# Two half stores of dV in uneven shares: some rows issued from GpSimd, with tiny loads that turn its cursor

## The chip, the cores and the metric

The kernel runs on one core of a Trainium2 chip. Its compute engines are TensorE (PE in the profile, with the weight loads as PEld), VectorE (DVE), ScalarE (ACT) and GpSimd (POOL); SyncE (SP) issues transfers and computes nothing. Sixteen DMA engines move data between HBM and the core's memory, whatever engine issued the transfer. The metric is the time of one execution in device microseconds, lower is better. A profiled execution gives, beside its time, a span (from the first to the last recorded instruction), the busy time of each engine and the records of the DMA packets.

## The reference

One query row attends to 8192 keys in each of 32 heads, and the gradients of all three inputs are wanted:

```python
B, H, Sq, Skv, Dh = 1, 32, 1, 8192, 128
scores = jnp.einsum('bhqd,bhkd->bhqk', q, k) * scale
attn = _softmax(scores, axis=-1)
out = jnp.einsum('bhqk,bhkd->bhqd', attn, v)
# outputs: out, dq, dk, dv  (vjp of the above with grad_out)
```

All arrays are bf16. K, V, dK and dV are 2 MB a head. With p the softmax row and ds the gradient of the scores, dV of a head is the outer product of p and grad_out, and dK that of ds and q. So 128 MB of K and V are read, and as much of dK and dV is written.

## The kernel before

The work goes head by head. A head's 8192 keys lie on 128 partitions, 64 keys each, so that one partition's part of a 2 MB tensor is a single run of 16 KB in HBM. A load of K or V (`load_k` L81, `load_v` L85) is one transfer of 128 rows of 16 KB.

For each head, in the loop at the end of the kernel: DVE transposes K in blocks (L162) and PE forms the scores (L177); softmax follows on DVE and ACT; PE transposes V (L197), ACT copies it out of PSUM (L188), and PE forms grad_out times V (L207). `contract` (L231) adds up the output and, with ds, dQ. `outer` (L256) writes dK and dV: DVE multiplies a repeated p or ds with a row, in four quarters of 16 keys per partition, into a tile of the pool `gen`, which holds two tiles each for dK and dV. After the fourth quarter, one transfer from SP stores all of it (L266); heads 0 and 31 store it in two halves. Iteration h of the loop does the scores and the softmax of head h, the dK of head h - 1 and the dV of head h.

K has three tiles and V two. K of head h + 2 is loaded once PE has finished the dQ of head h - 1 (the wait is on L231), V of head h + 2 once PE has read V of head h (L197 and L231). In the program the V load stands between the third and the fourth quarter of dV, and SP takes its transfers strictly in that order:

```python
        outer(h, "dv", 2)
        if 0 < h and h + 2 < H:
            load_v(h + 2)
        outer(h, "dv", 3)
```

The order is written out by hand (`manual_schedule`), and only the waits are added from what each instruction reads and writes. Eight completion semaphores go round over the transfers of SP and ACT, so that a transfer also waits for the one that had its semaphore before it. A tile of `gen` is written again two heads later, once its store has landed. GpSimd does a few memsets at the start and nothing else; all transfers are issued from SP, but for two small loads from ACT. At the very end the output and dQ are stored (`result`, L302).

Of the kernel before, what the change touches and what calls it, by code (L numbers as in the profile page):

```python
# [11 lines left out]
BF16 = mybir.dt.bfloat16  # L12
# [7 lines left out]
K_BUFS = 3  # L20
V_BUFS = 2
QD = 32


@with_exitstack
def kernel(
# [11 lines left out]
    nc = tc.nc  # L38
    P = 128
# [3 lines left out]
    NCH = NT // CH  # L43
    NQ = P // QD
    assert NCH == 4 and NQ == 4
    W = D // 2
    NB = W // QD
    scale = float(D) ** -0.5

    consts = ctx.enter_context(tc.tile_pool(name="consts", bufs=1))  # L50
# [18 lines left out]
    def rows_of(x, h, c, parts):  # L69
        L = NT // parts  # L70
        return x[0, h].rearrange("(p n) d -> p n d", p=P)[:, c * L:(c + 1) * L, :]

    def slots(X, c, parts):
        L = NT // parts
        return X[:, c * L:(c + 1) * L, :]

    def load_k(h):
        Kt[h] = kpool.tile([P, NT, D], BF16, tag="K", name="Kt")
        parts = NCH if h == 0 else 1
        for c in range(parts):  # L80
            nc.sync.dma_start(slots(Kt[h], c, parts), rows_of(k, h, c, parts))  # L81

    def load_v(h):
        Vt[h] = vpool.tile([P, NT, D], BF16, tag="V", name="Vt")
        nc.sync.dma_start(Vt[h][:], rows_of(v, h, 0, 1))  # L85
# [5 lines left out]
    load_v(0)  # L91
    load_k(1)
    load_v(1)

    ident = consts.tile([P, P], BF16)
    make_identity(nc, ident[:])
# [5 lines left out]
    nc.vector.memset(ones_f[:], 1.0)  # L102
    do_win = consts.tile([P, H, 2, QD + 2], BF16)
    nc.gpsimd.memset(do_win[:], 0.0)
    wins = {}
    for which in ("p", "ds"):
        wins[which] = []
        for i in range(2):
            w = consts.tile([P, NG, 2 * QD - 4], BF16, name=f"win_{which}{i}")
            nc.gpsimd.memset(w[:], 0.0)  # L110
            wins[which].append(w)
    q_win = []
    for i in range(2):
        w = consts.tile([P, 2 * NB, P + QD], BF16, name=f"win_q{i}")
        nc.gpsimd.memset(w[:], 0.0)
# [5 lines left out]
    q_blk = consts.tile([P, H, 2 * NB, NQ], BF16)  # L121
    four = consts.tile([H, 2 * NB, NQ, QD], BF16)
    for w in range(NB):
# [116 lines left out]
    def gather(h, which, bank):  # L240
# [5 lines left out]
                             start=(j == 0), stop=(j == 3), skip_group_check=True)  # L246
        nc.scalar.copy(to[:, h - ST + 1:h + 1], bank[:, at:at + ST])

    def outer(h, which, r):
        x = st[h]  # L250
        if r == 0:
            x[which] = gpool.tile([P, NT, D], BF16, tag=which, name="G_" + which)
        G, dst = x[which], out_2 if which == "dk" else out_3
        rep, row = x["ds"] if which == "dk" else x["p"], qd[h][:, 0 if which == "dk" else 1, :]
        Q = NT // 4
        nc.vector.tensor_tensor(  # L256
            slots(G, r, 4).rearrange("p n (a b) -> p n a b", b=R),
            slots(rep, r, 4).unsqueeze(2).to_broadcast([P, Q, D // R, R]),
            row.rearrange("p (a b) -> p a b", b=R).unsqueeze(1).to_broadcast([P, Q, D // R, R]),
            op=ALU.mult)  # L260
        parts = 1
        if h == 0 or h == H - 1:
            parts = 2
        if r % (4 // parts) == 4 // parts - 1:
            c = r // (4 // parts)
            nc.sync.dma_start(rows_of(dst, h, c, parts), slots(G, c, parts))  # L266
# [37 lines left out]
    for h in range(H + 1):  # L304
# [18 lines left out]
        if h > 0:  # L323
            ds_of(p_)
            outer(p_, "dk", 0)
            dq_of(p_, 0)
        if h < H:
            s_back(h)
        if h > 0:
            dq_of(p_, 1)  # L330
            outer(p_, "dk", 1)
            if p_ % ST == ST - 1:
                gather_copy("ds")
                gather(p_, "ds", st[p_]["m"])
# [9 lines left out]
        if h > 0:  # L344
            outer(p_, "dk", 2)
# [83 lines left out]
```

## Time and profile before

| | |
|---|---|
| time, median of 3 runs | 642.42 us (642.1 to 642.49) |
| the profiled execution's own time | 642.33 us |
| its span | 640.5 us |
| moved by DMA | 269.01 MB, mean 420 GB/s |
| DVE busy | 546.7 us (85%) |
| PE busy | 466.5 us (73%) |
| ACT busy | 205.5 us (32%) |
| POOL busy | 7.1 us (1%) |
| a 2 MB dV store, issue to landing | 34.8 us (median) |
| a 2 MB K load, issue to landing | 31.6 us (median) |

Busy time is the time in which an instruction of the engine ran; a DMA share is the mean over the sixteen DMA engines, so that one engine alone makes 0.06. "Landing" is when the last of a transfer's sixteen shares has arrived; the trace holds a completion record for each share, 4 bytes long, so that one can see how far apart the engines finish one transfer. The chain of waits is followed back from the last instruction to what released it. A 2 MB transfer puts eight rows of 16 KB on each DMA engine, and each engine works through its own queue.

### The profile page before, as it was taken

Reading aid. Unit: us, or ns where it says so; the run is one execution under the profiler, and the core shown is the slowest. Engines: PE = TensorE matmul, PEld = TensorE weight load, DVE = VectorE, ACT = ScalarE, POOL = GpSimd, SP = SyncE. Lnnn points to the kernel's source line nnn. Section 1 sums busy time; section 2 is a strip of 40 time slices with the busy share of each in tenths; the row PEclk is TensorE's granted clock in tenths of the full one; section 3 lists DMA queues with packets and bytes.
Section 4 is the critical chain, followed back from the end, with each engine's and each line's share of the span. In section 5 each row is a group of like instructions: output and inputs, shape, how many; then the busy total and the mean of one; then the engine's idle time right before and its main releaser. Section 6 shows DMA issues by size and latency. Waiting matters only on the chain.

```text
span 640.5 us, 8426 instructions
## 1 busy us (share of the span) xinstructions
PE 466.5 (73%) x3336; PEld 276.5 (43%) x3336; DVE 546.7 (85%) x780; ACT 205.5 (32%) x507; POOL 7.1 (1%) x13
## 2 busy tenths in 40 slices
PE   3776778778877867887866867767877687676771
PEld 1444444445544533455533444434554344444351
DVE  6799999998999999988889888898888988889871
ACT  1433332234433322334421333313442133322240
POOL 4000000000000000000000000000000000000000
PEclk9979888887787899877899887898787888879875
DMA  8999999999999999999999999999999999999994
GB/s 353 421 415 427 429 431 426 425 433 426 429 431 427 429 431 427 430 429 429 431 427 432 428 425 437 427 424 436 428 425 435 428 426 434 426 430 433 427 405 193
DMA packets 19671, 269.01 MB, mean 420 GB/s; under 512 B 2352, under 2 KB 2352, under 8 KB 2864
## 3 DMA queue, kind: packets, MB, share of 16 engines
q1 hardware_dynamic: 19536, 268.46, 98.6%
q8 instruction: 26, 0.43, 0.3%
q14 instruction: 13, 0.11, 0.0%
q10 hardware_dynamic: 96, 0.02, 0.0%
HBM read 134.23 MB, written 134.23 MB: 419 GB/s over the span
## 4 chain that ended last, share of the span: by engine, by line
DMA 45%; DVE 39%; PE 9%; ACT 4%; issue 1%; DVEq 0%; ACTq 0%
DMA Kt<-in_k_dram 45%; DVE XK_sb L162 15%; DVE G_dv L256 9%; DVE G_dk L256 7%; PE s_ps L177 3%; DVE dpT L214 2%; PE T_ps L197 2%; PE acc_ds L231 2%; ACT XV_sb L188 2%; DVE sT L184 1%; ACT p_rep L371 1%; DVE prod L217 1%; DVE ds L285 1%; ACT qd L273 1%; DVE four L125 1%
## 5 line engine op out<-in xcount | busy, mean ns | idle before, releaser
L197 PE MATMUL T_ps<-ident_f,Vt 128*128 128x128 f32 x1024 | 178.0, 339 | 1.0 <-DMA Vt<-in_v_dram 0.4
L256 DVE TENSOR_TENSOR G_dv<-p_rep,qd 128x2048 bf16<-128x2048 bf16 x128 | 148.2, 1220 | 35.3 <-DMA out_dram<-G_dv 28.1
L177 PE MATMUL s_ps<-XK_sb,win_q 128*128 128x512 bf16 x512 | 135.8, 397 | 50.1 <-DVE XK_sb L162 26.3
L197 PEld LDWEIGHTS T_ps<-ident_f,Vt 128*128 128x128 f32 x1024 | 151.4, 177 | 28.5 <-issue 20.1
L256 DVE TENSOR_TENSOR G_dk<-ds_rep,qd 128x2048 bf16<-128x2048 bf16 x128 | 154.7, 1210 | 1.1
L188 ACT COPY XV_sb<-T_ps 128x512 f32<-128x512 f32 x256 | 138.4, 586 | 53.2 <-PE T_ps L197 52.6
L162 DVE STREAM_TRANSPOSE XK_sb<-Kt 128x1024 f32<-128x1024 f32 x128 | 151.4, 1221 | 3.1 <-DMA Kt<-in_k_dram 2.9
L177 PEld LDWEIGHTS <-win_q 128*128 128x128 bf16 x512 | 52.7, 105 | 123.8 <-issue 83.2
L290 ACT COPY win_ds<-ds 128x64 bf16<-128x64 bf16 x32 | 7.8, 244 | 193.0 <-DVE ds L285 193.0
L355 ACT ACTIVATE e<-sT,nbias 128x64 f32<-128x64 f32 x32 | 13.0, 406 | 138.4 <-DVE nbias L350 138.4
L343 PE MATMUL m_ps<-ident_f,top 128*128 128x128 f32 x32 | 11.0, 342 | 60.3 <-DVE top L341 57.3
L207 PE MATMUL dp_ps<-XV_sb,do_win 128*32 128x512 bf16 x512 | 34.0, 382 | 24.7 <-ACT XV_sb L188 24.7
L231 PE MATMUL acc_p<-Vt,win_p 128*32 128x512 bf16 x512 | 48.3, 516 | 0.5 <-ACT win_p L372 0.5
L343 PEld LDWEIGHTS m_ps<-ident_f,top 128*128 128x128 f32 x32 | 4.5, 139 | 74.4 <-DVE top L341 72.9
L231 PE MATMUL acc_ds<-Kt,win_ds 128*32 128x512 bf16 x512 | 33.5, 382 | 0.9 <-ACT win_ds L290 0.9
L207 PEld LDWEIGHTS <-do_win 128*32 128x32 bf16 x512 | 14.2, 94 | 36.0 <-issue 29.5
L369 DVE RECIPROCAL rinv<-m_ps 128x1 f32<-128x1 f32 x32 | 5.4, 168 | 24.9 <-ACT qd L273 24.9
L184 DVE STREAM_TRANSPOSE sT<-s_ps 128x512 f32<-128x512 f32 x32 | 22.7, 709 | 3.6 <-PE s_ps L177 3.6
L356 PE MATMUL m_ps<-rs,ones_f 128*128 128x1 f32 x64 | 15.4, 310 | 11.5 <-ACT e L355 11.5
L231 PEld LDWEIGHTS <-win_p 128*32 128x32 bf16 x512 | 13.1, 117 | 23.8 <-issue 12.2
L214 DVE STREAM_TRANSPOSE dpT<-dp_ps 128x512 f32<-128x512 f32 x32 | 21.6, 675 | 0.8 <-PE dp_ps L207 0.8
L356 PEld LDWEIGHTS m_ps<-rs,ones_f 128*128 128x128 f32 x64 | 14.0, 272 | 17.8 <-ACT e L355 17.3
(57 smaller groups left out, 203.3 us busy)
## 6 DMA issues: line engine op xcount, KB each, us to landing
Vt<-in_v_dram SPq DMA_DIRECT2D x32, 2048.0 KB, 29.5
Kt<-in_k_dram SPq DMA_DIRECT2D x31, 2048.0 KB, 31.6
out_dram<-G_dv SPq DMA_DIRECT2D x30, 2048.0 KB, 34.8
out_dram<-G_dk SPq DMA_DIRECT2D x30, 2048.0 KB, 32.2
out_dram<-G_dv SPq DMA_DIRECT2D x4, 1024.0 KB, 11.6
out_dram<-G_dk SPq DMA_DIRECT2D x4, 1024.0 KB, 11.7
Kt<-in_k_dram SPq DMA_DIRECT2D x4, 512.0 KB, 5.6
out_dram<-fin_sb SPq DMA_DIRECT2D x2, 8.0 KB, 12.1
```

Of the source, the lines that this page charges most:

```text
L162: nc.vector.transpose(XK[h][:, :, :, u, :], slots(Kt[h], u, NCH).rearrange("p g d -> p (g d)").bitcast(F32).rearrange("p (g w j) -> p g w ...
L177: nc.tensor.matmul(st[h]["s"][:], lhsT=q_win[h % 2][:, c, at:at + P], rhs=cols[:, c // 2, u, c % 2], start=(u == 0 and c == 0), stop=(u == ...
L184: nc.vector.transpose(sT[:].rearrange("p g r -> p (g r)"), x["s"][:])
L188: nc.scalar.copy(XV[h][:, c * TB:(c + 1) * TB, :], st[h].pop(("T", c))[:])
L197: nc.tensor.transpose(T_ps[:, i, :], words[:, m * P:(m + 1) * P], ident_f[:])
L207: nc.tensor.matmul(out[b * QD:(b + 1) * QD, :], lhsT=do_win[:, h, e2, 2 - 2 * z:2 - 2 * z + QD], rhs=cols[:, z, e2, :, b * QD:(b + 1) * QD ...
L214: nc.vector.transpose(x["dpT"][:].rearrange("p m r -> p (m r)"), x["dp"][:])
L231: nc.tensor.matmul(acc[which][b * QD:(b + 1) * QD, :], lhsT=window(h, which)[:, g, at:at + QD], rhs=X[:, 4 * g:4 * g + 4, :].rearrange("p ...
L256: nc.vector.tensor_tensor(slots(G, r, 4).rearrange("p n (a b) -> p n a b", b=R), slots(rep, r, 4).unsqueeze(2).to_broadcast([P, Q, D // R, ...
L343: nc.tensor.transpose(x["m"][:, 128:256], top[:].to_broadcast([P, P]), ident_f[:])
L355: nc.scalar.activation(e[:].rearrange("p (u g) -> p u g", u=NCH), x["sn"], ACT.Exp, bias=nbias[:], scale=scale, accum_out=rs[:])
L356: nc.tensor.matmul(x["m"][:, 0:1], lhsT=ones_f[:], rhs=rs[:], start=True, stop=True, skip_group_check=True)
```

## The change

dV of heads 10 and 16 is no longer stored in one transfer after its fourth quarter. Its first half (L256's first two quarters) is stored from SP as soon as it is there, as 128 rows of 8 KB. The second half goes in pieces, named by rows (partitions) in the table `UNEVEN`. For head 10: rows 0 to 56 from SP, 57 to 94 and 95 to 127 from GpSimd. For head 16: rows 0 to 119 from GpSimd, 120 to 123 and 124 to 127 from SP. Between them GpSimd issues loads of a few bytes per row into a tile that nobody reads, of 7 and 12 rows at head 10 and of 5 and 12 at head 16 (`turn`). GpSimd's stores are cut into pieces of at most 4096 bytes. The bytes stored and all computing instructions stay what they were.

```diff
+UNEVEN = {
+    10: (("sync", 0, 57), ("turn", 7, 0), ("pool", 57, 95), ("turn", 12, 0), ("pool", 95, 128)),
+    16: (("turn", 5, 0), ("pool", 0, 120), ("turn", 12, 0), ("sync", 120, 124), ("sync", 124, 128)),
+}
...
+    turns = list(range(8))
+    turned = consts.tile([16, len(turns), 2, 2], BF16)
...
+    def turn(n):
+        i = turns.pop()
+        nc.gpsimd.dma_start(turned[0:n, i], k[0, 0].rearrange("(p n) d -> p n d", p=P)[0:n, 0:2, 0:2])
+
+    def spread(h, c, dst, G):
+        if c == 0:
+            nc.sync.dma_start(rows_of(dst, h, 0, 2), slots(G, 0, 2))
+            return
+        for what, a, b in UNEVEN[h]:
+            if what == "turn":
+                turn(a)
+            elif what == "sync":
+                nc.sync.dma_start(rows_of(dst, h, 1, 2)[a:b], slots(G, 1, 2)[a:b])
+            else:
+                nc.gpsimd.dma_start(rows_of(dst, h, 1, 2)[a:b], slots(G, 1, 2)[a:b], max_dma_last_dim=4096)
...
             op=ALU.mult)
+        if which == "dv" and h in UNEVEN:
+            if r % 2 == 1:
+                spread(h, r // 2, dst, G)
+            return
         parts = 1
```

## The prediction

> **What bounds the kernel now.** I read the page's DMA rows first, then the chain, then the DMA share by stretch, then the trace's completion records of single transfers.
>
> ```profile
> span 640.5 us, 8426 instructions
> ...
> DMA  8999999999999999999999999999999999999994
> ...
> q1 hardware_dynamic: 19536, 268.46, 98.6%
> q8 instruction: 26, 0.43, 0.3%
> ...
> DMA 45%; DVE 39%; PE 9%; ACT 4%; issue 1%; DVEq 0%; ACTq 0%
> ```
>
> The DMA engines are full in every slice but the first and the last. DVE, the busiest compute engine, is at 85%. The chain runs over DVE in its first part and from 251.94 us on over K loads of some 32 us each, one for two heads: early on the kernel lives on loads made ahead, later on what the DMA engines deliver. The trace's packets say how full: a 16 KB row takes 611 ns (median), an 8 KB row 309, a 4 KB one 159, a completion record of 4 bytes 9, and from 20 to 600 us sixteen packets, one per engine, are under way all the time. So an engine with more to do, or a slower one, ends later, and nothing evens that out. The share by stretch shows that this is so at the end (columns: stretch, its length, the engines' busy time, the TensorE clock, DMA share, GB/s):
>
> ```profile
> 400.00:600.00 200.00, 147.53 (x1052) 86.68 (x1052) 170.52 (x242) 63.34 (x156) 0.00 (x0) 0.86 1.01 429
> 600.00:616.00 16.00, 11.83 (x74) 6.40 (x74) 13.23 (x22) 4.10 (x10) 0.00 (x0) 0.83 1.01 431
> 616.00:625.00 9.00, 6.17 (x58) 4.44 (x58) 6.95 (x11) 3.62 (x9) 0.00 (x0) 0.88 0.90 375
> 625.00:631.00 6.00, 1.69 (x8) 1.40 (x8) 2.45 (x3) 0.64 (x3) 0.00 (x0) 0.50 0.96 399
> 631.00:632.00 1.00, 0.00 (x0) 0.00 (x0) 0.00 (x0) 0.00 (x0) 0.00 (x0) 0.50 0.50 203
> 632.00:634.00 2.00, 0.00 (x0) 0.00 (x0) 0.00 (x0) 0.00 (x0) 0.00 (x0) 0.50 0.24 99
> 634.00:636.00 2.00, 0.00 (x0) 0.00 (x0) 0.00 (x0) 0.00 (x0) 0.00 (x0) 0.50 0.12 50
> 636.00:639.00 3.00, 0.00 (x0) 0.00 (x0) 0.00 (x0) 0.00 (x0) 0.00 (x0) 0.50 0.06 25
> ```
>
> The last three shares are four, two and one sixteenth: from 636 us a single engine works, and everything waits for it. The sixteen completion records of the last transfer (the dQ store, issued at 627.90) agree: twelve at 631.59 to 632.39, then 634.35, 635.19, 635.72 and 639.47. The dV store of head 30 (issued at 599.24), where no engine has yet run dry, sorts the engines better: five at 612.91 to 613.60, one at 615.34, six at 617.25 to 617.62, three at 619.80 to 620.96, one at 624.51. Five fast, ten between, one slow, 11.6 us behind the first. The slow one loses steadily: about 0.15 us at each 2 MB store and 0.03 at each load. The middle ones lag in steps of some 1.45 us, one at each of the 26 instruction packets of q8; the fast ones show almost none.
>
> The lag also reaches the compute. K of head 31 lands last on the slow engine, and the work of that head follows:
>
> ```profile
> 567.39 31.98 DMA Kt<-in_k_dram
> 599.40 3.50 DVE XK_sb L162 x3
> ```
>
> Its records run from 588.58 to 596.62 for fifteen engines, and to 599.38 for the last one.
>
> **The change part by part.** *Where the rows go.* The two second halves give every engine 16 rows of 8 KB before (two halves, 128 rows each, 8 on each of 16 engines, as every 128-row transfer of the trace has 16 completion records). How a count that 16 does not divide is shared out, no row of this trace shows. The bounds: at most those 16 rows leave an engine, 16 x 0.309 = 4.94 us; at most one engine takes the largest single transfer that need not be even, 57 rows, 57 x 0.309 = 17.6 us, less the 16 it had, 12.7 us more. Both ends are kept for the rivals. The value I take comes from the counts themselves: 57 + 38 is 5 x 19, 33 is 11 x 3, 120 is 15 x 8, 4 is 4 x 1; shares of equal size on as many engines as divide the count. I read SP's transfers as starting at engine 0 and `turn(n)` as moving GpSimd's cursor by n, from 0. Head 10: SP's 57 rows put 19 on engines 0, 1, 2; the cursor at 7 puts 19 on 7 and 8; at 9 + 12 = 21, that is 5, the 33 put 3 on each of 5 to 15. Head 16: from 5 on, 8 rows on fifteen engines, all but 4; SP's two fours put one row twice on 0 to 3. Against the 16 of before: engines 0 to 2 +13, 7 and 8 +14, engine 3 -6, 5, 6 and 9 to 15 -5, engine 4 -16. Five get more, ten a little less, one far less: the same five, ten and one as in the records. I cannot see engine numbers there, but this match is why I take engine 4 for the slow one and the value near the lower bound.
>
> *The slow engine:* 16 rows less, -4.94 us, 639.47 to 634.53. *The next three:* -5 rows, -1.55 us, 635.72 to 634.17; they stay just under. *The five fast:* +14 x 0.309 = 4.33 us. They run dry at the end (share 0.90 at 616 to 625): after 617.75 they have four 1 MB stores left, 32 x 0.309 = 9.9 us, so even without a pause they end at 617.75 + 9.9 + 4.3 = 632, under 634.5. *Compute:* K of head 31 lands at the later of 599.38 - 4.94 = 594.44 and 596.62 - 1.55 = 595.07, 4.3 us sooner; the last stores are issued by about 623.2 instead of 627.5 and do not decide.
>
> *Smaller rows:* the first halves go as 8 KB rows, 309 ns for what was 611 / 2 = 305.5: 16 x 3.5 ns = 0.06 us on each engine. GpSimd's rows are cut into two 4 KB pieces, 318 for 309: 0.2 us on engines 7 and 8 alone. *The four tiny loads:* a few pieces of 4 bytes on an engine, between 9 ns (completion record) and 18 ns (256-byte row): under 0.1 us.
>
> *GpSimd's issue.* POOL is idle after 7.6 us, and the seven transfers stand at its end with a wait on DVE at the first store of each head; nobody queues behind. Making such a transfer has no row here: between the 0.33 us of an SP issue and the 1.92 us of POOL's longest instruction, for each of two or three. It is hidden, as the rows are needed only when the buffer comes round two heads later: dV of head 10 is issued at 209.29, and head 12 first writes the buffer at 239.8. By the lag at 233 us (fast 0, slow 5.04) engines 0 to 2 with 11 rows more in that half land it at 233.2 + 3.4 = 236.6, still in time. If that cover fails, DVE waits; a few us at head 12 are given back, since the engines still hold some 30 us of work.
>
> *SP.* The first half is issued before the V load of head h + 2 instead of behind it: V lands 8 x 0.309 = 2.5 us later. V of head 12 landed at 233.4 and is first used at 236.1, so that is covered; V of head 18 landed at 351.3 and is used at 351.4, so PE waits some 2.4 us there, and the queues go on meanwhile. One transfer more at head 10 and two at 16: eight completion semaphores go round, so each transfer waits for the one eight places before it. After head 16 I get, by the landings of before: the second four-row store waits for dK of 14 (326.6 against 321.6), K of 19 is issued at 331.5 instead of 329.4, dV of 17 at 346.4 instead of 341.3. The engines then still hold 15 us or more of queued rows (V of 19 lands from 364.7 on), so 0 on the path; were the queue to run dry, up to 5 us.
>
> The sum, on the profiled execution's own 642.33 us (span 640.5), 0.09 under the median 642.42: -4.94 + 0.06 + 0.1 = -4.8, **637.5 us**.
>
> Against it stands a rule of the Trainium skill, page "DMA: Bandwidth & Descriptors", "Rules for kernel authors": spreading transfers over issuing engines gains no bandwidth, as all run on the same 16. By it alone the sum would be 0 and the time 642.4; but the tail row at 0.06 share is not one of bandwidth, it is one engine's own queue.
> The same page, "Why a DMA increments its semaphore by 16", says that the largest divisor up to 16 sets the number of engines, lowest first from SP and from a round-robin cursor on GpSimd, with a measured exception for some GpSimd copies, shared out over all 16; by the exception the cursor would do nothing and engine 4 lose 2 rows, 641.7. Its "Latency and other measured facts" calls engines 7 and 15 usually slower; were 7 the slow one, +14 rows would give 646.7. No row here numbers the engines.
>
> **The rivals.**
> - *The slow engine is one of the five that get more* (cursor or numbers not as I read them). For: no engine number is in the trace. Against: the five, ten and one. +13 to +14 rows: 639.47 + 4.0 to 4.3, so 646.4 to 646.7, slower (the far end, +12.7 us, would be 655). It decides as soon as the slow engine takes 5 rows more than before (1.5 us).
> - *The slow engine is in the middle group:* -5 rows, 640.9; or one of the next three gets +14: 635.72 + 4.33 = 640.1, which is no longer the end unless its step falls later. 640 to 643.
> - *The counts come out nearly even,* the cursor has no effect: one or two rows either way, 641.7 to 642.7.
> - *A stall:* the semaphore turn or a late buffer lets the queues run dry; 2 to 5 us on top of no gain, 643.5 to 647.
>
> **How the numbers follow.** A measurement of this kernel can tell about 0.2%, 1.3 us. As read: 0.64, 636.4 to 638.8 (the next three unrelieved would give 642.4 - 3.75 = 638.7). Middle group: 0.14, of it 0.08 faster, 0.03 same, 0.03 slower. Slow engine loaded: 0.12, slower. Even: 0.06, of it 0.02 faster, 0.04 same. Stall: 0.04, slower. Faster 0.74, same 0.07, slower 0.19. From 636.4 to 643.3 lie the first, the second and the fourth, 0.84.
>
> **What would show it.** Right: the DMA share falls off around 631 to 634.5 with no stretch of 3 us at 0.06; the latest record of head 30's dV is about 6.7 us behind the first five's old place, not 11.6; K of 31 lands near 595. Wrong: a longer lone tail after 636, or the same one; DVE waiting on the dV stores of 10 or 16; a DMA share under 0.9 anywhere in 200 to 600.

## The result, and the profile after

The changed kernel takes 639.53 us (median of 6 runs, 639.15 to 639.86) where the kernel before took 642.45 beside it. The ratio is 0.9955, interval 0.9942 to 0.9968: 2.9 us faster, where 4.9 were forecast. The profiled execution took 639.71 us with a span of 637.9; before it was 642.33 and 640.5, so that it shows 2.6 us.

From the page of the changed kernel, the span, the DMA engines' busy share in 40 slices, the queues (packets, MB, share of sixteen engines) and the shares of the chain of waits:

```profile
span 637.9 us, 8444 instructions
...
DMA  8999999999999999999999999999999999999996
...
q1 hardware_dynamic: 19612, 266.90, 98.5%
q0 software_dynamic: 1136, 1.57, 0.7%
q8 instruction: 26, 0.43, 0.2%
...
DMA 41%; DVE 39%; PE 11%; ACT 5%; issue 1%; POOL 0%; DVEq 0%; ACTq 0%
```

The DMA engines are as full as before. Queue q0 is new and is GpSimd's: 1.57 MB, the 191 rows of 8 KB of its three stores, 382 pieces of 4 KB; the other 754 of its packets are of 4 or 8 bytes. The other engines do what they did. The last slice rose from 4 to 6 tenths: the end is sharper.

The DMA share by stretch at the end of the changed kernel (columns as in the prediction):

```profile
600.00:616.00 16.00, 12.14 (x95) 7.55 (x96) 13.22 (x22) 6.06 (x14) 0.00 (x0) 0.89 1.01 429
616.00:625.00 9.00, 6.06 (x44) 3.85 (x36) 7.75 (x12) 1.85 (x7) 0.00 (x0) 0.63 0.99 422
625.00:631.00 6.00, 0.24 (x1) 0.05 (x1) 0.00 (x0) 0.25 (x1) 0.00 (x0) 0.50 0.93 389
631.00:632.00 1.00, 0.00 (x0) 0.00 (x0) 0.00 (x0) 0.00 (x0) 0.00 (x0) 0.50 0.55 231
632.00:634.00 2.00, 0.00 (x0) 0.00 (x0) 0.00 (x0) 0.00 (x0) 0.00 (x0) 0.50 0.32 132
634.00:636.00 2.00, 0.00 (x0) 0.00 (x0) 0.00 (x0) 0.00 (x0) 0.00 (x0) 0.50 0.12 50
636.00:639.00 3.00, 0.00 (x0) 0.00 (x0) 0.00 (x0) 0.00 (x0) 0.00 (x0) 0.50 0.01 3
```

From 636 us on a share of 0.06, one engine, has become 0.01. But in 632 to 634 it is 0.32, five sixteenths, where it was 0.24: more engines end late. The completion records of the dV store of head 30, as us behind the first of its sixteen engines, show the whole field (from the traces; first 612.91 before, 612.82 after):

```
before 0.00 0.04 0.07 0.09 0.69 2.43 4.34 4.51 4.64 4.68 4.70 4.71 6.89 7.54 8.05 11.60
after  0.00 2.30 2.33 2.43 3.38 4.17 4.34 4.38 4.86 4.95 5.36 6.17 7.09 7.90 7.92  9.31
```

Of the five engines that came first one leads alone, the others have joined the middle, and the 11.60 is gone. The last place, 9.31, belongs to another engine. It can be followed from transfer to transfer by its steps at four instruction packets (28, 208, 401 and 591 us), and before it was one of the next three. On the last transfer (dQ) it ends at 636.91; the formerly slow engine ends at about 635.83 there, and at 639.47 before.

Two lines of the chain of waits after, K of head 31 and the work that follows it:

```profile
565.20 32.62 DMA Kt<-in_k_dram
597.84 3.50 DVE XK_sb L169 x3
```

Its load was issued 2.19 us sooner than before (565.20 for 567.39) but took 32.62 us instead of 31.98, and landed 1.6 us sooner (597.82 for 599.38).

### The profile page after: what moved, and what is told of

The parts are those of the page before. It is cut to its first block, busy times and chain, and to the rows that moved or that the text cites. A ratio compares the mean times of both kernels' runs of the same rounds, so it can differ in the third digit from the quotient of the medians.

```text
span 637.9 us, 8444 instructions
## 1 busy us (share of the span) xinstructions
PE 470.7 (74%) x3336; PEld 277.4 (43%) x3336; DVE 546.7 (86%) x780; ACT 205.5 (32%) x507; POOL 11.7 (2%) x20
## 3 DMA queue, kind: packets, MB, share of 16 engines
q0 software_dynamic: 1136, 1.57, 0.7%
## 4 chain that ended last, share of the span: by engine, by line
DMA 41%; DVE 39%; PE 11%; ACT 5%; issue 1%; POOL 0%; DVEq 0%; ACTq 0%
DMA Kt<-in_k_dram 29%; DVE XK_sb L169 13%; DVE G_dv L279 11%; DVE G_dk L279 8%; DMA out_dram<-G_dv 5%; DMA Vt<-in_v_dram 5%; PE s_ps L184 4%; PE T_ps L204 3%; ACT XV_sb L195 2%; DVE dpT L221 2%; DVE sT L191 2%; PE acc_ds L238 1%; ACT p_rep L398 1%; PE m_ps L383 1%; PE acc_p L238 1%
## 5 line engine op out<-in xcount | busy, mean ns | idle before, releaser
L184 PE MATMUL s_ps<-XK_sb,win_q 128*128 128x512 bf16 x512 | 138.4, 410 | 40.4 <-DVE XK_sb L169 23.4
L238 PE MATMUL acc_p<-Vt,win_p 128*32 128x512 bf16 x512 | 51.0, 540 | 0.9 <-ACT win_p L399 0.9
L214 PEld LDWEIGHTS <-do_win 128*32 128x32 bf16 x512 | 14.2, 94 | 36.0 <-issue 29.4
L238 PEld LDWEIGHTS <-win_p 128*32 128x32 bf16 x512 | 13.4, 120 | 25.3 <-issue 14.2
## 6 DMA issues: line engine op xcount, KB each, us to landing
Kt<-in_k_dram SPq DMA_DIRECT2D x31, 2048.0 KB, 30.8
out_dram<-G_dv POOLq DMA_DIRECT2D x1, 960.0 KB, 18.3
```

The source lines that it names most:

```text
L184: nc.tensor.matmul(st[h]["s"][:], lhsT=q_win[h % 2][:, c, at:at + P], rhs=cols[:, c // 2, u, c % 2], start=(u == 0 and c == 0), stop=(u == ...
L214: nc.tensor.matmul(out[b * QD:(b + 1) * QD, :], lhsT=do_win[:, h, e2, 2 - 2 * z:2 - 2 * z + QD], rhs=cols[:, z, e2, :, b * QD:(b + 1) * QD ...
L238: nc.tensor.matmul(acc[which][b * QD:(b + 1) * QD, :], lhsT=window(h, which)[:, g, at:at + QD], rhs=X[:, 4 * g:4 * g + 4, :].rearrange("p ...
```

## The experiments

All kernels store everything that the changed kernel stores; they differ in the table `UNEVEN`, but for one with another piece size. The kernel before ran beside each of them, with medians of 642.45 to 642.54. Where "long packets" are given, the length of every packet above the median length of its size (611 ns for 16 KB, 309 for 8, 159 for 4, 9 for a completion record) is summed over the sixteen engines, instruction packets left out, in three stretches of the trace: 205 to 255 us (after head 10's store), 320 to 360 (head 16's), 438 to 490 (head 22's). The last record and the long packets are those of the one profiled execution, whose time is up to 0.9 us off the kernel's median; the same store of head 10 shows 10.2 to 17.5 us of long packets in five traces, so that smaller differences say little. "Slow engine" is the one that was last before.

| kernel | median us | ratio (interval) | last record, dQ | long packets, us |
|---|---|---|---|---|
| before | 642.45 | | 639.47 | 3.8 / 2.8 / 2.9 |
| changed kernel | 639.53 | 0.9955 (0.9942 to 0.9968) | 636.91 | 10.2 / 15.2 / 2.5 |
| head 10 alone | 640.07 | 0.9959 (0.9947 to 0.9972) | 637.61 | 16.2 / 2.6 / 2.0 |
| head 16 alone | 640.40 | 0.9966 (0.9954 to 0.9979) | 637.51 | 3.0 / 22.8 / 2.1 |
| GpSimd, 128 rows | 642.15 | 0.9994 (0.9985 to 1.0003) | 639.39 | 9.0 / 1.8 / 2.0 |
| engine 5 left out | 641.87 | 0.9990 (0.9981 to 0.9999) | 639.00 | 3.3 / 13.8 / 2.2 |
| two halves from SP | 641.58 | 0.9986 (0.9978 to 0.9995) | 638.98 | 5.7 / 1.9 / 1.9 |
| pieces of 8 KB | 642.04 | 0.9994 (0.9985 to 1.0002) | 639.83 | 33.3 / 15.2 / 2.1 |
| uneven from SP | 641.70 | 0.9991 (0.9982 to 1.0) | 639.37 | 2.8 / 3.5 / 2.6 |
| two skips | 640.84 | 0.9975 (0.9966 to 0.9984) | 638.38 | 28.9 / 24.3 / 2.5 |
| 64 + 64 rows from GpSimd | 643.32 | 1.0016 (1.0007 to 1.0026) | 640.27 | 24.8 / 17.2 / 2.0 |
| changed kernel again | 640.12 | 0.9958 (0.9946 to 0.9971) | 637.49 | 13.7 / 11.6 / 2.5 |
| head 22 for head 16 | 639.42 | 0.9951 (0.9938 to 0.9963) | 636.59 | 16.4 / 2.6 / 10.3 |
| head 10's way twice | 640.06 | 0.9968 (0.9957 to 0.998) | 638.14 | 17.5 / 2.6 / 8.0 |

### One head at a time

```diff
 UNEVEN = {
     10: (("sync", 0, 57), ("turn", 7, 0), ("pool", 57, 95), ("turn", 12, 0), ("pool", 95, 128)),
-    16: (("turn", 5, 0), ("pool", 0, 120), ("turn", 12, 0), ("sync", 120, 124), ("sync", 124, 128)),
 }
```

> Only head 10 is stored unevenly; head 16 as before. Theory A (the lone slow engine sheds 8 rows of 309 ns a head, 2.47 us; part of the gain is lost to packets that run longer than 611 ns around the GpSimd stores): the slow engine still ends last, 642.4 - 2.5 + 0.4 = 640.3 us. Rival B (GpSimd's way of storing has a fixed price of some 0.95 us a head, whatever it relieves): 642.4 - 2.5 + 0.95 = 640.9. Rival C (another engine takes over as the last as soon as the slow one is relieved by 8 rows): one head brings as much as both, 639.5.

And head 16 alone:

```diff
 UNEVEN = {
-    10: (("sync", 0, 57), ("turn", 7, 0), ("pool", 57, 95), ("turn", 12, 0), ("pool", 95, 128)),
     16: (("turn", 5, 0), ("pool", 0, 120), ("turn", 12, 0), ("sync", 120, 124), ("sync", 124, 128)),
 }
```

> Only head 16 is stored unevenly; head 10 as before. Theory A: the slow engine sheds 2.47 us; the packets around the stores of head 16 were longer by some 12 us summed over 16 engines, 0.7 us each, so 642.4 - 2.5 + 0.7 = 640.6 us, and in the records around 330 to 345 us the long packets come again. Rival B: 640.9, with no long packets. Rival C: 639.5.

The DMA share by stretch, head 10 alone:

```profile
634.00:636.00 2.00, 0.00 (x0) 0.00 (x0) 0.00 (x0) 0.00 (x0) 0.00 (x0) 0.50 0.09 37
636.00:639.00 3.00, 0.00 (x0) 0.00 (x0) 0.00 (x0) 0.00 (x0) 0.00 (x0) 0.50 0.02 8
```

Head 16 alone:

```profile
634.00:636.00 2.00, 0.00 (x0) 0.00 (x0) 0.00 (x0) 0.00 (x0) 0.00 (x0) 0.50 0.12 49
636.00:639.00 3.00, 0.00 (x0) 0.00 (x0) 0.00 (x0) 0.00 (x0) 0.00 (x0) 0.50 0.01 6
```

Either head takes 8 rows, 2.47 us by the rows, from the slow engine, and either gains about that: 2.38 and 2.05 us. In both the slow engine still comes last, at 637.61 and 637.51, 1.9 to 2.0 us sooner than before. Together they would be worth 4.4, near the forecast; the changed kernel gains 2.9. So each part does its work, and the second one finds less left to win: another engine ends then.

### Which engine is relieved

Head 16 alone, with the cursor one place further, so that engine 5 is left out of the 120 rows and engine 4 isn't:

```diff
-    16: (("turn", 5, 0), ("pool", 0, 120), ("turn", 12, 0), ("sync", 120, 124), ("sync", 124, 128)),
+    16: (("turn", 6, 0), ("pool", 0, 120), ("turn", 11, 0), ("sync", 120, 124), ("sync", 124, 128)),
```

> Head 16 alone as in the run of head 16 alone, but the cursor is turned one further (by 6, and by 11 afterwards), so that engine 5 is left out of the 120 rows and engine 4 has its 8. If engine 4 is the slow one (theory A): no relief, 642.4 + 0.7 = 643.1 us, and the last records stay some 11.6 us behind the first. If the slow engine's number is not known by this (rival: any engine left out would do, or the slow one is 5): 640 to 640.6.

```profile
634.00:636.00 2.00, 0.00 (x0) 0.00 (x0) 0.00 (x0) 0.00 (x0) 0.00 (x0) 0.50 0.13 54
636.00:639.00 3.00, 0.00 (x0) 0.00 (x0) 0.00 (x0) 0.00 (x0) 0.00 (x0) 0.50 0.05 19
```

These are its last two stretches: at 636 to 639 us 0.05 for the 0.01 of head 16 alone. The slow engine ends at 639.00, and the time is 641.87 against 640.40. One place of the cursor is worth 1.5 us, so the slow engine is the one that `turn(5)` spares. The expectation had 643.1 us for this case; why it is 0.6 us faster than before, and not 0.7 slower, stays open. The Trainium skill, page "DMA: Bandwidth & Descriptors", section "Why a DMA increments its semaphore by 16 and not by 1", has GpSimd's shares on consecutive engines from a round-robin cursor, and SP's on the lowest; on that numbering it is engine 4. Its section "Latency and other measured facts" calls 7 and 15 usually slower; no run here shows that.

### GpSimd without uneven shares

```diff
-    10: (("sync", 0, 57), ("turn", 7, 0), ("pool", 57, 95), ("turn", 12, 0), ("pool", 95, 128)),
-    16: (("turn", 5, 0), ("pool", 0, 120), ("turn", 12, 0), ("sync", 120, 124), ("sync", 124, 128)),
+    10: (("pool", 0, 128),),
+    16: (("pool", 0, 128),),
```

> The second halves of heads 10 and 16 go from GpSimd as 128 rows each, 8 on every engine: the GpSimd way without any shift of rows. Theory A: no relief, and only the longer packets: 642.4 + 0.5 to 1.1 = 642.9 to 643.5 us. Rival B: the price of the way alone, 642.4 + 1.9 = 644.3. If the loss in the changed kernel came from the uneven shares and not from GpSimd: 642.4 to 642.6.

642.15 us, within what can be told from no change and under what any of the expectations had, and the slow engine ends at 639.39, as before. The issuing engine alone gives nothing; the gain is in the counts. This is what the rule in the Trainium skill's "Rules for kernel authors" (same page) says of spreading transfers over issuing engines, and the changed kernel's 2.9 us are no breach of it: no stretch before the end moves more bytes.

### SP without GpSimd

The second halves from SP as one transfer of 128 rows each, and the same for head 16 in 68 + 60 rows, which leaves fewer rows on the engines behind the fourth:

```diff
-    10: (("sync", 0, 57), ("turn", 7, 0), ("pool", 57, 95), ("turn", 12, 0), ("pool", 95, 128)),
-    16: (("turn", 5, 0), ("pool", 0, 120), ("turn", 12, 0), ("sync", 120, 124), ("sync", 124, 128)),
+    10: (("sync", 0, 128),),
+    16: (("sync", 0, 128),),
```

> Heads 10 and 16 stored from SP in two halves of 128 rows each, 8 rows a half on every engine; no GpSimd, no uneven shares. Shows what the split, the V load behind the first half and the extra turn of the semaphores cost by themselves. Theory A (the loss comes from longer packets around the GpSimd store of head 16 and from another engine ending last): 642.4 to 642.6 us, no cluster of packets over 1 us near 330 us. Rival C2 (the split and the delayed issues on SP cost the missing time): 643 to 644.4.

```diff
-    10: (("sync", 0, 57), ("turn", 7, 0), ("pool", 57, 95), ("turn", 12, 0), ("pool", 95, 128)),
-    16: (("turn", 5, 0), ("pool", 0, 120), ("turn", 12, 0), ("sync", 120, 124), ("sync", 124, 128)),
+    16: (("sync", 0, 68), ("sync", 68, 128)),
```

> Head 16's second half from SP alone in uneven shares, 68 rows and 60 rows: read as 17 rows on each of engines 0 to 3, then 4 on each of engines 0 to 14; so engine 4 sheds 4 rows, 1.24 us, and engines 0 to 3 take 13 more. Theory A: no GpSimd, no cluster of long packets, 642.4 - 1.24 = 641.2 us. If uneven shares by themselves make the packets long: 641.7 to 642.2.

The last two stretches of the uneven one:

```profile
634.00:636.00 2.00, 0.00 (x0) 0.00 (x0) 0.00 (x0) 0.00 (x0) 0.00 (x0) 0.50 0.12 49
636.00:639.00 3.00, 0.00 (x0) 0.00 (x0) 0.00 (x0) 0.00 (x0) 0.00 (x0) 0.50 0.09 39
```

The two halves give 0.9 us, which none of the theories has. The profiled execution has fewer long packets than before (43.9 us over sixteen engines from 20 to 620 us, for 52.8), 4.8 us of the difference ahead of head 10 where the programs are the same; that doesn't explain a median over many runs. It stays open. The changed kernel stores its first halves in the same way, so part of its 2.9 us may be this and not the counts; the split with GpSimd's 128 rows gave 0.3. 68 + 60 rows put 17 on engines 0 to 3, 4 on 4 to 14. The slow engine has 4 rows less, 1.24 us by the rows, and a record of the dV store of head 30 at 623.29, for its 624.51 before, fits that to 0.02. But another engine is then last there, at 624.58. The median gains 0.8 us, of which the profiled execution (642.17 us, last record 639.37) shows little. Less 13 x 0.309 = 4.0 that engine would stand at 620.6, among the next three of before (619.80 to 620.96): one of engines 0 to 3 is not of the leading five. The change loads only 0 to 2 and relieves 3.

### Where the long packets come from

In the table they come with the uneven stores from GpSimd, at the head where these stand, and not with the uneven ones from SP (3.5) nor, at head 16, with 128 rows from GpSimd (1.8). Three kernels ask why. The first cuts GpSimd's rows into pieces of 8 KB:

```diff
-                nc.gpsimd.dma_start(rows_of(dst, h, 1, 2)[a:b], slots(G, 1, 2)[a:b], max_dma_last_dim=4096)
+                nc.gpsimd.dma_start(rows_of(dst, h, 1, 2)[a:b], slots(G, 1, 2)[a:b], max_dma_last_dim=8192)
```

> The changed kernel with GpSimd's rows as one 8 KB piece instead of two of 4 KB: half as many pieces taken in turn with SP's 16 KB rows. If the many small pieces make the neighbours' packets long (the cluster near 330 us): fewer long packets, 638.5 to 639.2 us. Theory A without a say on the size: 639.5, within 0.4.

What the DMA engines moved in each of the 40 slices of its span, in GB/s:

```profile
GB/s 352 418 431 431 428 426 427 432 427 430 429 427 426 376 428 430 430 432 428 431 424 411 430 427 428 434 428 427 434 427 428 433 426 432 430 431 433 427 419 224
```

The 14th slice (208 to 224 us), in which head 10's store begins, falls to 376 GB/s, from 426 to 430 around it. The gain is gone (642.04 us), against both expectations. But this run changes more than the size of the pieces: it deals the rows out otherwise. From its page and its DMA issues (KB, us to landing):

```profile
q0 software_dynamic: 400, 1.57, 0.6%
out_dram<-G_dv POOLq DMA_DIRECT2D x1, 304.0 KB, 8.3
```

The 304 KB (38 rows) land after 8.3 us instead of 30.8, and seven of their pieces are under way at once within 0.5 us of the first; in the changed kernel it is never more than two before 232 us. The packets of 4 bytes on q0 say how the rows lie. There are 145 of them, in the changed kernel 690. Sixteen completion records for each of the seven transfers make 112. The rest fits one filler packet for each piece by which an engine has fewer than the fullest one. With 4 KB pieces and the prediction's shares that is 14 x 38 + 5 x 6 + 16 = 578, and 690 in all. With 8 KB pieces it fits shares over all sixteen engines, 3, 3 and 8 rows on each as far as they go: 10 + 15 + 8 = 33, and 145 in all. The same count gives the 626, 64 and 1252 of head 10 alone, head 16 alone and head 10's way twice. So with 8 KB pieces the slow engine isn't spared: by these shares it sheds 2 rows and not 16, for which the prediction had 641.7 us. The run can't say what the size of the pieces does by itself.

The second sends the second halves of both heads from GpSimd as 64 + 64 rows. Every engine has as many rows and bytes as before, 4 + 4 instead of 8, but, as the expectation reads it, other rows than in a transfer of 128 (no record names an engine's rows):

```diff
-    10: (("sync", 0, 57), ("turn", 7, 0), ("pool", 57, 95), ("turn", 12, 0), ("pool", 95, 128)),
-    16: (("turn", 5, 0), ("pool", 0, 120), ("turn", 12, 0), ("sync", 120, 124), ("sync", 124, 128)),
+    10: (("pool", 0, 64), ("pool", 64, 128)),
+    16: (("pool", 0, 64), ("pool", 64, 128)),
```

> The second halves of heads 10 and 16 from GpSimd in two transfers of 64 rows each: every engine still gets 8 rows a half, but not the rows that it has in a transfer of 128. Theory D1 (packets get long because an engine reads rows that in the other transfers belong to another engine): long packets as in the changed kernel, over 8 us above the nominal lengths summed over the engines at 200 to 250 and again at 320 to 350 us, time 642.5 to 643.5. Theory D2 (because GpSimd's shares are unequal): like the 128-row run, under 9 and under 3 us, 641.8 to 642.4.

The GB/s per slice of GpSimd with 128 rows, and then of 64 + 64:

```profile
GB/s 350 423 405 432 430 427 429 429 427 431 427 428 428 429 417 434 428 429 433 429 426 433 429 428 434 428 429 432 430 429 430 431 428 430 429 430 432 428 413 191
```

```profile
GB/s 350 422 426 428 431 425 430 427 429 426 427 429 429 416 404 428 430 430 429 430 412 420 430 428 433 428 428 431 429 431 430 427 432 428 432 429 428 434 412 206
```

The slices to compare are the 14th and 15th (head 10) and the 21st and 22nd (head 16): 429 417 and 426 433 with 128 rows, 416 404 and 412 420 with 64 + 64. The kernel is 0.8 us slower than before, with even shares. So uneven counts are not needed for the long packets. Rows on other engines than usual may be what is enough, but that is not shown: this kernel also has two transfers from GpSimd at each head instead of one, and the 68 + 60 rows from SP lie on other engines than usual too, with 3.5 us. The 405 in the 3rd slice of the first line stands ahead of any such store: a cluster between 40 and 50 us, which other kernels have too and which reaches 14.2 us (the repetition of the changed kernel) without any such store. Nor do the long packets only lie beside GpSimd's pieces: with 64 + 64 rows 12.7 of head 10's 24.8 us fall in 230 to 240 us, and the last piece starts before 226. What makes them long is not settled.

The third keeps head 10 and gives head 16's table to head 22:

```diff
-    16: (("turn", 5, 0), ("pool", 0, 120), ("turn", 12, 0), ("sync", 120, 124), ("sync", 124, 128)),
+    22: (("turn", 5, 0), ("pool", 0, 120), ("turn", 12, 0), ("sync", 120, 124), ("sync", 124, 128)),
```

> Head 10 as in the changed kernel, and head 16's way moved to head 22, whose dV is issued near 440 us. Theory A (the long packets belong to the GpSimd store in 15 shares, wherever it stands): they show at 440 to 470 us and not at 320 to 350, and the time is that of the changed kernel, 639.5 within 0.5. If they belong to the place (head 16's neighbours): none at either, and 638.3 to 639.

The long packets go along: 2.6 us at head 16's place and 10.3 at head 22's. 639.42 us is not to be told from the changed kernel, whose repetition is the next run:

> The changed kernel once more, for a second trace beside the others of this call. Theory A: 639.5 us; again an engine other than the slow one has the last completion record, the long packets are there again at 320 to 350 us, and the mean landing of K of head 31 is 0.5 to 1 us later than before (592.5). If the take-over in the first trace was chance: the slow engine is last and the mean within 0.3 us.

640.12 us, again with an engine other than the slow one last: records of dQ at 635.07, 636.04, 636.18 and 637.49. K of head 31 lands at 594.0 in the mean, 1.5 us later than before, more than the 0.5 to 1 expected.

### Who ends then

Head 16's way at both heads takes the same 16 rows from the slow engine as the change, but none from the next three (engines 0 to 3 get 4 more, 5 to 15 what they had):

```diff
-    10: (("sync", 0, 57), ("turn", 7, 0), ("pool", 57, 95), ("turn", 12, 0), ("pool", 95, 128)),
+    10: (("turn", 5, 0), ("pool", 0, 120), ("turn", 12, 0), ("sync", 120, 124), ("sync", 124, 128)),
```

> Heads 10 and 16 both stored in the way of head 16: 8 rows on every engine but engine 4, and two more on engines 0 to 3. The slow engine sheds 16 rows as in the changed kernel (4.94 us), but the middle engines get no relief at all. Theory A (another engine ends last once the slow one is relieved): the engine next behind, at 635.7 before, decides, 642.4 - 3.75 + 0.7 to 1.5 = 639.4 to 640.2 us, no better than the changed kernel and little better than head 16 alone (640.4). Rival (each head's relief counts in full): 642.4 - 2 x 2.05 = 638.3.

```profile
634.00:636.00 2.00, 0.00 (x0) 0.00 (x0) 0.00 (x0) 0.00 (x0) 0.00 (x0) 0.50 0.44 185
636.00:639.00 3.00, 0.00 (x0) 0.00 (x0) 0.00 (x0) 0.00 (x0) 0.00 (x0) 0.50 0.09 36
```

These are its last two stretches: from 634 to 636 us seven sixteenths are still at work, one or two after. Four engines end within 1.2 us of each other (637.16 to 638.38), and the gain is 1.7 us instead of 2.9; 640.84 us is past the 640.2 of theory A, and far from its rival's 638.3. The slow engine's relief is worth only the way to the next engine. Whether the 5 rows less on the others make the rest of the changed kernel's gain is not shown: the long packets here sum up to 53.2 us at the two heads instead of 25.4, 1.7 us more for a mean engine, and this kernel is only 1.3 us slower than the changed one.

If the end goes to whichever engine is then last, more relief for the middle should move the end to the loaded engines. Head 10's way at heads 10 and 22, head 16 as before:

```diff
-    16: (("turn", 5, 0), ("pool", 0, 120), ("turn", 12, 0), ("sync", 120, 124), ("sync", 124, 128)),
+    22: (("sync", 0, 57), ("turn", 7, 0), ("pool", 57, 95), ("turn", 12, 0), ("pool", 95, 128)),
```

> Head 10's way of storing at heads 10 and 22, head 16 stored as before. By the counts, against the kernel before: the slow engine and its neighbour 16 rows less, the ten in between 10 less instead of 5, the five others 22 more. Theory (the end is whatever engine is then last, and the changed kernel ends with a middle one that was relieved too little): from the run with head 10 alone, where the last transfer's records end at 633.28, 635.43 and 637.61, the slow engine falls by 8 x 0.309 = 2.47 to 635.1, the middle one by 5 x 0.309 = 1.55 to 633.9, and a loaded engine rises by 11 x 0.309 = 3.4 to at most 636.7; long packets around the second store add some 0.6 us to all. The last record is then between 635.7 and 637.3, and the time, which lies 2.8 us behind it, 638.5 to 640.1: no later than the changed kernel's 639.5 by more than 0.6, and with a middle engine no longer last. Rival (long packets at each such store eat what a further relief gives): a second cluster of 10 us or more, over sixteen engines, pushes all of them, the middle one stays last and the time is 640.1 to 641, as with head 10 alone or later.

```profile
634.00:636.00 2.00, 0.00 (x0) 0.00 (x0) 0.00 (x0) 0.00 (x0) 0.00 (x0) 0.50 0.32 136
636.00:639.00 3.00, 0.00 (x0) 0.00 (x0) 0.00 (x0) 0.00 (x0) 0.00 (x0) 0.50 0.06 23
```

The stretches are of an execution of 641.0 us, 0.9 over the median of 640.06: five engines at work from 634 to 636 (0.32), one after. The records of the dV store of head 30 behind the first, at 613.11:

```
0.00 0.95 1.02 1.30 1.84 2.37 2.68 3.58 3.94 5.83 7.06 8.55 8.56 8.80 9.57 10.14
```

Now five come last, at 621.66 to 623.25, where before five came first. With 22 x 0.309 = 6.8 us more, the counts put the first five (612.91 to 613.60 before) at 619.7 to 620.4 and the one 2.43 behind at 622.1; measured are some 1 to 3 us more. The middle ones stand at 614.1 to 615.8; the counts gave 617.25 to 617.62, less 10 x 0.309, so 614.2 to 614.5. So the end went where the counts send it, as the theory had it; the time, at the upper end of its 638.5 to 640.1, did not improve, as the loaded engines overshoot. The rival's second cluster of 10 us or more was 8.0 us, and no middle engine was last.

No kernel here is clearly faster than the changed one.

## Why the prediction was right, and where its size failed

**Where the rows go** held. SP's 57 rows left three completion records over time, its fours four each. The issues of the uneven stores in the changed kernel (KB, us to landing):

```profile
out_dram<-G_dv POOLq DMA_DIRECT2D x1, 960.0 KB, 18.3
out_dram<-G_dv SPq DMA_DIRECT2D x1, 456.0 KB
out_dram<-G_dv POOLq DMA_DIRECT2D x1, 304.0 KB, 30.8
out_dram<-G_dv POOLq DMA_DIRECT2D x1, 264.0 KB, 35.0
```

In the packets, the 120 rows are sixteen pieces of 4 KB on each of fifteen engines and none on the sixteenth, the 38 rows lie on two engines and the 33 on eleven. The Trainium skill's rule of the largest divisor (the section named above) agrees with this. Its exception of sixteen shares did not appear for 38, 33 or 120 rows in pieces of 4 KB, so the rival of nearly even counts falls; but the same rows in pieces of 8 KB fit it. That the shares came as read hung on the limit of 4096 bytes on a piece; the prediction named the exception, but not this as what decides, and that part is luck. The records do not number the engines; the cursor moved by one place is what settled that the spared one is the slow one, and the rivals "one of the five" and "in the middle group" fall with it. One detail was off: the group 0, 1, 2, 7, 8 isn't quite the five leading engines. By their steps at instruction packets, one of the leading five was relieved and leads alone now (0.00, then 2.30), and the one that was 2.43 behind was loaded.

**The slow engine**: 4.94 us were forecast, 639.47 to 634.53. It ended at about 635.83, 3.64 sooner. Its rows were taken as read; the missing 1.3 us is near the 1.2 that longer packets cost a mean engine (below), and which no term of the sum had. That this is the cause is argued, not shown: ahead of head 10 the trace has 7.1 us less of long packets than before (19.7 for 26.8), so that over 20 to 620 us the sums are only 7.6 us apart, 0.5 for a mean engine.

**The next three** is the step that failed: "they stay just under", 635.72 to 634.17. One of them ends last, at 636.91, 1.2 us later than before instead of 1.55 sooner. Its rows did go down, or it would have come far behind in the run with head 10's way twice (22 rows more would put it at about 627 on head 30's dV, where the last is at 623.25). Strung together packet by packet, as an engine's next packet begins where its last one ends, it carries six of head 10's 4 KB pieces and sixteen of head 16's, three and eight rows, as counted. It got longer packets: these grew by 6.4 + 12.4 = 18.8 us in the stretches of heads 10 and 16, 1.2 us for a mean engine; its own are some 4 us over their nominal lengths there, and it fell back some 1.5 us behind the first around head 16's store alone. The 64 + 64 run shows such clusters without any change of the counts, at 0.8 us of the time. How its 2.7 us divide is not resolved, and why the packets get long stays open. The time follows it: 636.91 for 639.47 is 2.56 us, and the profiled execution is 2.62 us shorter.

**"The five fast"** did not decide, as forecast: the counts put them at about 617 on head 30's dV, where ten of the records lie between 615.1 and 618.2, and the engine that is last is none of them. Given 22 rows instead of 14, they decide.

**Compute** came less early: K of head 31 at 597.82, 1.6 sooner for the 4.3 forecast, and dQ was issued at 625.55 (2.35 sooner). It did not set the end.

**GpSimd's issue** was in its bounds. The issues of one store each took 0.62 to 1.02 us, and the loads of the turns 0.56 to 0.68; nothing was queued behind. The cover behind it failed. Head 10's dV was to land by 236.6, ahead of the first write at 239.8, but the last of its stores took 35.0 us (the chain of waits):

```profile
209.35 35.02 DMA out_dram<-G_dv
244.55 4.63 DVE G_dv L279 x4
```

DVE waited 4.4 us for it at head 12, which was one of the prediction's signs of being wrong. As the prediction said of that case, the engines had work queued: the DMA share stayed at 1.01 from 220 to 300 us, and the wait cost nothing at the end. The sum for the landing had SP's 19 rows in it, and not that GpSimd's pieces are taken in turn with 16 KB rows: on two engines the 38 and the 33 rows put 44 pieces, and 44 x (0.159 + 0.611) = 33.9 us.

**SP**: K of head 19 was issued at 331.4 (331.5 forecast), dV of 17 at 350.1 (346.4 forecast), and V of 18 landed 6.1 us later than before (357.4 for 351.3) where 2.5 were forecast. These waits were longer than worked out, and cost nothing at the end, as the DMA engines stayed full; the rival of a stall falls. **Smaller rows** is too small to be seen, but overlooked that a piece taken in turn with a 16 KB row may make that row long. **The four tiny loads** had "a few pieces of 4 bytes on an engine"; with GpSimd's filler packets and records there are 754 small packets, 47 for a mean engine and 69 on the one that gets no rows. At 6 ns from one's start to the next packet's that is 0.3 and 0.4 us, an estimate, for the under 0.1 forecast.

So the time lies in the range of 636.4 to 643.3, and 0.7 above the 638.8 to which the case as read reached: the direction and the mechanism (one engine's own queue sets the end, and fewer rows on it end it sooner) were right, and the size was 0.6 of the forecast. That it lies in the range is in part luck: the range was stretched over the middle-group and even rivals, which both fall, and 639.53 lies between the case as read and the 640 at which the first of them begins. In that rival, 635.72 + 4.33 = 640.1 is a time in the trace, past the 639.47 of before; it would have been the end, and some 642.9 us. Of the signs of being right, only the shorter lone tail came as stated: the last record of head 30's dV came 9.2 us behind the first five's old place instead of 6.7, and K of head 31 at 597.8 instead of near 595.

## What to carry to other kernels

When the last stretches of a profile show one sixteenth of the DMA share, read the completion records of one late transfer: they order the engines, and unequal row counts then buy time. Only the way to the next engine can be won, so sum the field after the change, all sixteen, with some slack for each (here 1 to 3 us), not the one that was last. A store from GpSimd in uneven or split shares had a price of its own here: try one of its kind without the gain (even counts, 64 + 64 rows) before trusting a sum of row times. And check in the trace on how many engines a transfer lies before building on its shares: here a limit on the size of its pieces changed that.

## What was not expected of the hardware

- Rows of 16 KB from SP take up to 2.2 us instead of 0.61 near such stores (2235 and 2085 ns at 332.6 and 333.1 us in the changed kernel), while TensorE, VectorE and the amount moved stay the same. Two even stores of 64 rows from GpSimd do it (24.8 and 17.2 us summed at heads 10 and 16), one of 128 rows does at head 10 but not at head 16 (9.0 and 1.8), uneven ones from SP don't (3.5 at head 16); before it is 3.8 and 2.8. The cause is open.
- An engine with GpSimd's pieces and SP's rows queued takes them in turn, one piece of 4 KB and one row of 16 KB. So the 304 KB store, 38 pieces on each of two engines, takes 30.8 us to land, and the 264 KB one 35.0, as it comes behind those pieces on the same two engines; the 960 KB one, 16 pieces on each of fifteen, takes 18.3.
- The limit on the size of a piece decides on how many engines GpSimd's rows lie: 38 rows of 8 KB lie on two engines in pieces of 4 KB and, by the count of small packets, on thirteen in pieces of 8 KB (642.04 us for 639.53).
- Uneven shares from GpSimd bring small packets to the engines with fewer pieces: 690 of 4 bytes in the changed kernel, 145 with pieces of 8 KB, 32 with even stores of 128 rows.
